# Experts' second product by Strassen's scheme in two of three super chunks

## The chip, the cores and the metric

The kernel runs on one core of one Trainium2 chip. The metric is the device time of one execution in microseconds (us); the median of three runs of the kernel before is 2102.27 us (2100.63 to 2102.86).

## The reference, cut to what matters

Feature attention (4 batches, 8 heads, 576 positions) gives x, a chain of matrix products turns x into a new x of 2304 tokens by 512, and a mixture of eight experts makes the output. The change touches the experts alone:

```python
P = np.exp(logits)                       # gate, then 8 rounds of row and column scaling
out = np.zeros((N, D), dtype=np.float32)  # N 2304 tokens, D 512, 8 experts of width F 1024
for e in range(E):
    h = np.maximum(x @ w1[e], 0.0)       # first product
    ye = h @ w2[e]                       # second product
    out += P[:, e:e + 1] * ye
```

## The kernel before, in words

Every float32 operand is kept as a high and a low part in the fast float32 format of TensorE, and each product of two tiles is three matmuls (high with high, high with low, low with high), written by `mm3` (L86). The attention, the product chain and the gate's logits fill the first 564 us; the experts fill the rest.

The 2304 tokens are cut into three super chunks (s) of 768 tokens, in two column halves of 384. Inside a super chunk the eight experts (e) follow each other, and in an expert four units (p). A unit makes two row blocks of 128 hidden values, p and p + 4, for 768 tokens.

The first product of a unit already uses Strassen's scheme (Winograd's form): seven products of 384 columns in place of eight, each of six matmuls (`product` in `unit`, L732). A product lands in a PSUM bank (pool `ph`, five banks); VectorE adds it into one of four 128 x 384 tiles of a buffer `c` (L749; two such buffers, pool `ut`); ScalarE copies the first one. `h_split` (L728) then takes relu and splits it into `hH` (ScalarE) and `hL` (VectorE).

The second product of an expert runs when its four units are done: for each of six tiles of 128 tokens, eight row blocks by three matmuls of 512 columns into a bank of pool `py`, 144 matmuls in all. VectorE multiplies the result by the gate and adds it to the output tile `oacc` (L857).

Weights: in the first super chunk `load_w1` and `prep_w1` (L482, L491) fetch the seven combinations of w1 for each unit, split them, and store the split form in a DRAM scratch (`W1S`, 1.79 MB a unit, counted in 1024s). In the two later super chunks that scratch is loaded again, into one of three buffers. w2 is loaded and split anew for every expert of every super chunk (`load_w2` L710, `split_w2` L719): ScalarE makes the high part, VectorE or GpSimd the low part. The x operands of the first product are made once per super chunk (`load_x`, `prep_x`, L450 and L454).

The order of instructions on each engine is planned when the program is built. The planner takes, of what it holds to be ready, the instruction that stands first in the program text; the adds of a product are moved 60 places forward. Engines run their lists in order, so an instruction that waits holds up all behind it. All large DMAs are issued by SP, in its own list.

Of the kernel before, what the change touches and what calls it, by code (L numbers as in the profile page):

```python
# [15 lines left out]
    Xl="v", Xs="g", Wt="v", Wh="a", Wl="gv", W2h="a", W2l="vg",  # L16
# [11 lines left out]
def kernel(  # L28
# [80 lines left out]
    W1S = [scr.tile([P, 2, 7, 2 * P], F32, name=f"w1s{i}") for i in range(NE * FT2 // 2)]  # L109
# [340 lines left out]
    def load_x(s):  # L450
        rawX[s] = rx.tile([P, KT, 2 * N1], F32, name=f"rx{s}", tag="rx")
        nc.sync.dma_start(rawX[s], XS[s])

    def prep_x(s):  # L454
        r = rawX.pop(s)
        a, b = slice(0, N1), slice(N1, 2 * N1)
        a11, a12, a21, a22 = r[:, 0:2, a], r[:, 2:4, a], r[:, 0:2, b], r[:, 2:4, b]
# [24 lines left out]
    def load_w1(u):  # L482
        if u < len(units):
# [4 lines left out]
            nc.sync.dma_start(rawW1[u][:, 0:3], moe2_w1[e, p][:, 1:4])  # L488
            nc.sync.dma_start(rawW1[u][:, 3:7], W1T[u])

    def prep_w1(u):  # L491
        if u >= len(units):
            return
        n = u % len(W1S)
        if u >= len(W1S):
            pool = wc1c[0] if u % 3 == 2 else wc1
            hl = pool.tile([P, 2, 7, 2 * P], F32R, name=f"w1_{u}", tag="hl")
            nc.sync.dma_start(f32(hl), W1S[n])
            WC[u] = hl[:, 0], hl[:, 1]
            return  # L500
        r = rawW1.pop(u)
        hl = wc1.tile([P, 2, 7, 2 * P], F32R, name=f"w1_{u}", tag="hl")
        hi, lo = hl[:, 0], hl[:, 1]
        for i, c in enumerate((slice(0, 3), slice(3, 7))):
            copy("Wh", hi[:, c], r[:, c], 2 * u + i)
            subtract("Wl", lo[:, c], r[:, c], f32(hi[:, c]), 2 * u + i)
        nc.sync.dma_start(W1S[n], f32(hl))
        WC[u] = hi, lo
# [188 lines left out]
    with c4:  # L697
        hp = sbuf(c4, "hp")
        ut = sbuf(c4, "ut", 2)
        op = sbuf(c4, "op")  # L700
        sk = sbuf(c4, "sk", 2)
        st = sbuf(c4, "st", 2)
        wp = sbuf(c4, "wp")
        ph_p = c4.enter_context(tc.tile_pool(name="ph", reuse_waits="tile", bufs=5, space=PSUM))
        py_p = c4.enter_context(tc.tile_pool(name="py", reuse_waits="tile", bufs=2, space=PSUM))
# [4 lines left out]
        def load_w2(u):  # L710
            if u < len(units):
# [3 lines left out]
                    t, moe2_w2[e, 2 * p * P : 2 * (p + 1) * P, :].rearrange("(j p) d -> p j d", p=P)  # L715
                )
                rawW2[u] = t

        def split_w2(u):  # L719
            s, e, p = units[u]  # L720
            t = rawW2.pop(u)
            hi = wp.tile([P, 2, DM], F32R, name=f"w2h{u}", tag=f"h{p}")
            lo = wp.tile([P, 2, DM], F32R, name=f"w2l{u}", tag=f"l{p}")
            copy("W2h", hi, t, u)
            subtract("W2l", lo, t, f32(hi), u)
            W2[p] = hi, lo

# [4 lines left out]
        def unit(u, between):  # L732
# [3 lines left out]
            B11, B21, B22, T1, T2, T3, T4 = range(7)  # L736

            def product(x, i, *adds):
                ps = ph_p.tile([P, N1], F32, name=f"p{x}{u}", tag="ph")
                (wh, wl), (xh, xl) = WC[u], XC[x]  # L740
                for kt in range(2):
                    k = slice(kt * P, (kt + 1) * P)
                    mm3(ps, wh[:, i, k], wl[:, i, k], xh[:, kt], xl[:, kt], kt == 0, kt == 1)
# [11 lines left out]
            product("s1", T1, (c22, c21), (c12, c12))  # L755
            product("a12", B21, (c11, c11))
            product("a22", T4, (c21, c21))
# [56 lines left out]
        for u, (s, e, p) in enumerate(units):  # L814

            if u + 1 < len(W1S):
                prep_w1(u + 1)
                load_w1(u + 2)
            if u + 2 == len(W1S):
                c6.close()  # L820
                wc1c.append(sbuf(c6, "wc1c", 1, "left"))
            if u + 2 >= len(W1S):
                prep_w1(u + 2)
# [5 lines left out]
            if e == 0 and s + 1 < NSC:  # L829
                load_x(s + 1)  # L830
            if e == NE - 1 and s + 1 < NSC:
                prep_x(s + 1)
            for tt in range(2 * N1 // P):
# [7 lines left out]
                for n, ft in enumerate(fts):  # L841
                    hi, lo = W2[ft // 2]
                    mm3(ps, hH[ft][:, tcs], hL[ft][:, tcs], hi[:, ft % 2], lo[:, ft % 2], n == 0, n == FT2 - 1)
# [14 lines left out]
                if e == NE - 1:  # L858
                    nc.sync.dma_start(out[t * P : (t + 1) * P, :], o)

# [75 lines left out]
```

## Time and profile before

| | |
|---|---|
| median of three runs | 2102.27 us |
| profiled execution, whole | 2102.98 us |
| its span, first to last instruction | 2101.2 us |
| TensorE busy | 2051.8 us (98%), 11877 matmuls |
| VectorE busy | 1131.7 us (54%) |
| ScalarE busy | 597.6 us (28%) |
| GpSimd busy | 361.4 us (17%) |
| granted TensorE clock, mean | 0.994 |
| DMA | 345 MB, 164 GB/s over the span |

Busy time of an engine is the time in which at least one of its instructions was in flight. Matmuls overlap, so the time from one start to the next tells what a matmul costs, and not its own duration. A row of a timeline names the engine, the line, the tile written and the tiles read; "x2" means two such instructions merged. A DMA share of 1.00 means that all 16 engines were at work.

### The profile page before, as it was taken

What the parts mean: (1) busy time and instruction counts of PE and PEld (TensorE: products, weight loads), DVE (VectorE), ACT (ScalarE), POOL (GpSimd) and SP (SyncE); (2) the same over time, 40 slices, a digit from 0 to 9 for tenths busy, and PEclk for the clock granted to TensorE, in tenths of its full rate; (3) what the DMA queues carried; (4) which work ended last, traced back from release to release, by engine and by line L of the source; (5) the groups of instructions that cost most, each with busy time, mean ns of one, the idle gap of its engine ahead of it and who ended that gap; (6) DMA issues with size and microseconds to landing.
All of it is one profiled execution on the core that took longest, in us unless ns stands there. A gap on an engine that the chain in (4) does not pass through costs nothing.

```text
span 2101.2 us, 28910 instructions
## 1 busy us (share of the span) xinstructions
PE 2051.8 (98%) x11877; PEld 1819.2 (87%) x11877; DVE 1131.7 (54%) x1718; ACT 597.6 (28%) x979; POOL 361.4 (17%) x268
## 2 busy tenths in 40 slices
PE   7999889999989999999999999999999999999999
PEld 6667689999978888889888999888999888999887
DVE  7765853343586554666554555444565443555443
ACT  6765532222333322233221122111132211122211
POOL 3433331221422211122120000000010000000000
PEclk9999999999999999999999999999999999999999
DMA  6432345554574545665464444333455333444330
GB/s 214 146 119 84 131 141 156 183 158 156 215 270 170 204 167 221 240 226 191 168 228 154 171 180 166 129 110 147 170 190 192 124 114 142 170 180 179 120 117 31
DMA packets 78531, 345.44 MB, mean 164 GB/s; under 512 B 7488, under 2 KB 11456, under 8 KB 65728
## 3 DMA queue, kind: packets, MB, share of 16 engines
q1 hardware_dynamic: 77808, 342.95, 45.7%
q8 instruction: 93, 1.52, 0.3%
q10 hardware_dynamic: 592, 0.66, 0.1%
q14 instruction: 38, 0.31, 0.0%
HBM read 256.54 MB, written 87.03 MB: 164 GB/s over the span
## 4 chain that ended last, share of the span: by engine, by line
PE 83%; DVE 6%; ACT 3%; issue 3%; POOL 3%; DMA 2%; ACTq 0%; SPq 0%; DVEq 0%; POOLq 0%
PE py L89 13%; PE py L87 13%; PE py L88 13%; PE ps L87 6%; PE ps L88 5%; PE ps L89 5%; PE pa L89 4%; PE pa L88 4%; PE pa L87 4%; PE ab L89 3%; PE ab L87 3%; PE ab L88 3%; DMA r<-in_moe_w_dram 1%; PE px L89 1%; PE px L88 1%
## 5 line engine op out<-in xcount | busy, mean ns | idle before, releaser
L89 PE MATMUL py<-w2h,hL 128*128 128x512 f32 x1152 | 457.5, 397 | 0.6 <-DVE hL L730 0.4
L87 PE MATMUL py<-w2h,hH 128*128 128x512 f32 x1152 | 456.7, 396 | 0.6 <-DVE o L855 0.6
L88 PE MATMUL py<-w2l,hH 128*128 128x512 f32 x1152 | 456.8, 397 | 0.0
L857 DVE SCALAR_TENSOR_TENSOR o<-py,Pw,o 128x512 f32<-128x512 f32 x126 | 94.6, 751 | 451.9 <-PE py L89 451.9
L99 POOL TENSOR_TENSOR w2l<-r,w2h 128x1024 fp32r<-128x1024 f32 x48 | 116.2, 2421 | 1106.3 <-ACT w2h L96 1093.0
L749 DVE TENSOR_TENSOR c<-c,ps 128x384 f32<-128x384 f32 x480 | 256.0, 549 | 88.1 <-PE ps L89 81.3
L96 ACT CAST w2h<-r 128x1024 fp32r<-128x1024 f32 x96 | 101.0, 1052 | 701.1 <-PE py L89 613.1
L89 PEld LDWEIGHTS py<-w2h,hL 128*128 128x128 f32 x1152 | 216.8, 188 | 56.5 <-DVE hL L730 4.3
L87 PEld LDWEIGHTS py<-w2h,hH 128*128 128x128 f32 x1152 | 217.0, 188 | 52.8 <-DVE o L855 1.0
L88 PEld LDWEIGHTS py<-w2l,hH 128*128 128x128 f32 x1152 | 217.0, 188 | 51.5
L730 DVE SCALAR_TENSOR_TENSOR hL<-c,hH 128x768 fp32r<-128x768 f32 x192 | 234.4, 1237 | 27.7 <-ACT hH L729 25.9
L729 ACT ACTIVATE hH<-c 128x768 fp32r<-128x768 f32 x192 | 158.0, 843 | 294.9 <-DVE c L749 273.1
L87 PE MATMUL ab<-XH,wH 128*128 128x384 f32 x384 | 131.2, 342 | 8.6 <-DVE wH L96 8.6
L89 PE MATMUL ab<-XH,wL 128*128 128x384 f32 x384 | 131.3, 342 | 1.1 <-DVE wL L99 1.1
L88 PE MATMUL ab<-XL,wH 128*128 128x384 f32 x384 | 130.7, 340 | 0.0
L749 DVE TENSOR_TENSOR c<-c,pa 128x384 f32<-128x384 f32 x192 | 102.2, 549 | 17.4 <-PE pa L89 16.0
L647 POOL TENSOR_TENSOR cL<-a,cH 128x384 fp32r<-128x384 f32 x48 | 58.3, 1215 | 232.2 <-ACT cH L646 232.1
L99 DVE TENSOR_TENSOR w2l<-r,w2h 128x1024 fp32r<-128x1024 f32 x48 | 60.3, 1257 | 58.7 <-ACT w2h L96 58.6
L99 POOL TENSOR_TENSOR w<-r,w 128x768 fp32r<-128x768 f32 x32 | 65.8, 2058 | 130.1 <-ACT w L96 114.0
L96 ACT CAST w<-r 128x768 fp32r<-128x768 f32 x64 | 59.8, 938 | 95.4 <-DMA r<-in_moe_w_dram 30.4
L645 DVE TENSOR_TENSOR a<-ab,a 128x384 f32<-128x384 f32 x48 | 26.7, 557 | 104.9 <-PE ab L89 104.9
L87 PEld LDWEIGHTS ab<-XH,wH 128*128 128x128 f32 x384 | 72.9, 190 | 10.2 <-DVE wH L96 8.3
(174 smaller groups left out, 3842.8 us busy)
## 6 DMA issues: line engine op xcount, KB each, us to landing
w<-w1s SPq DMA_DIRECT2D x64, 1792.0 KB, 7.5
w1s<-w SPq DMA_DIRECT2D x32, 1792.0 KB, 6.6
r<-in_moe_w_dram SPq DMA_DIRECT2D x96, 512.0 KB, 3.5
rw<-in_w_dram SPq DMA_DIRECT2D x32, 512.0 KB, 3.8
tr<-in_moe_w_dram SPq DMA_DIRECT2D x32, 512.0 KB, 4.4
w1t<-tt SPq DMA_DIRECT2D x32, 512.0 KB, 5.1
r<-w1t SPq DMA_DIRECT2D x32, 512.0 KB, 8.2
r<-in_moe_w_dram SPq DMA_DIRECT2D x32, 384.0 KB, 7.7
```

What stands on the lines that cost most here:

```text
L87: nc.tensor.matmul(ps, aH, bH, start=start, stop=False)
L88: nc.tensor.matmul(ps, aH, bL, start=False, stop=False)
L89: nc.tensor.matmul(ps, aL, bH, start=False, stop=stop)
L96: (e.copy if e is nc.scalar else e.tensor_copy)(out, src)
L99: engine(key, i).tensor_tensor(out, a, b, ALU.subtract)
L645: behind = nc.vector.tensor_tensor(cc, ab[1], a_sb, ALU.mult).ins
L647: nc.gpsimd.tensor_tensor(l, cc, f32(h), ALU.subtract)
L729: nc.scalar.activation(hH[ft], src, AF.Relu)
L730: nc.vector.scalar_tensor_tensor(hL[ft], src, 0.0, f32(hH[ft]), ALU.max, ALU.subtract)
L749: nc.vector.tensor_tensor(o, t, ps, ALU.add)
L857: nc.vector.scalar_tensor_tensor(o, ps, Pw[:, t, e : e + 1], o, ALU.mult, ALU.add)
```

## The change

In the second and third super chunks the second product is computed by Strassen's scheme as well: h is the left factor, cut in four blocks (two halves of the tokens, two halves of the hidden rows), w2 is the right factor. Seven groups of products on half-size blocks replace eight. A group is four units by three token tiles by three matmuls of 256 columns. VectorE and ScalarE form the combinations of h after each unit (`operands`); the combinations of w2 are formed and split once, in the first super chunk (`split_w2`), stored in a DRAM scratch `W2S`, and loaded group by group in the later ones (`load_t`, three buffers). Partial results are copied out by ScalarE (`keep`) and added to the output by VectorE (`gated`). The first super chunk itself computes as before, with w2's row blocks paired p and p + 4. The split w1 is kept in two tiles (five and two combinations) with two buffers of each in place of three whole ones; `back_w1` reloads each part as soon as the unit two earlier has finished reading it. The x of the third super chunk is loaded into the two `c` buffers.

The core of the diff:

```diff
-    Xl="v", Xs="g", Wt="v", Wh="a", Wl="gv", W2h="a", W2l="vg",
+    Xl="v", Xs="g", Wt="v", Wh="a", Wl="vgg", W2h="a", W2l="vg", Tw="v", Th="a", Tl="v",
...
+    W2S = [scr.tile([P, 7, FT2 // 2, 2, DH], F32, name=f"w2s{i}") for i in range(NE)]
...
+    def back_w1(u, i):
+        if len(W1S) <= u < len(units):
+            if i == 1:
+                w1_tiles(u)
+            nc.sync.dma_start(f32(WC[u][1 - i]), W1S[u % len(W1S)][i])
...
         def split_w2(u):
...
             copy("W2h", hi, t, u)
             subtract("W2l", lo, t, f32(hi), u)
             W2[p] = hi, lo
+            for k, j, d in ((K11, 0, d0), (K21, 1, d0), (K22, 1, d1)):
+                nc.sync.dma_start(W2S[e][:, k, p], f32(w[:, j, :, d]))
+            add("Tw", b11, b12, b11, ALU.subtract)
+            add("Tw", b12, b22, b12, ALU.subtract)
+            add("Tw", b22, b11, b22, ALU.subtract)
+            add("Tw", b21, b21, b22, ALU.add)
+            x = tp.tile([P, 4, 2, DH], F32R, name=f"t2_{u}", tag="t")
+            copy("Th", x[:, :, 0], t, u)
+            subtract("Tl", x[:, :, 1], t, f32(x[:, :, 0]), u)
+            for i, k in enumerate((KT1, KT3, KT4, KN2)):
+                nc.sync.dma_start(W2S[e][:, k, p], f32(x[:, i]))
...
-            product("a12", B21, (c11, c11))
             product("a22", T4, (c21, c21))
-            h_split(p, c[:, 0:2].rearrange("p a n -> p (a n)"))
+            back_w1(u + 2, 1)
+            product("a12", B21, (c11, c11))
+            yield c
             product("s4", B22, (c12, c12))
-            h_split(p + NP, c[:, 2:4].rearrange("p a n -> p (a n)"))
+            back_w1(u + 2, 0)
+            yield c
...
+        def split(u, key, n, src, relu):
...
+            if relu:
+                nc.scalar.activation(hi, src, AF.Relu)
+                nc.vector.scalar_tensor_tensor(lo, src, 0.0, f32(hi), ALU.max, ALU.subtract)
+            else:
+                nc.scalar.copy(hi, src)
+                nc.vector.tensor_tensor(lo, src, f32(hi), ALU.subtract)
+        def operands(u):
+            for i, c in enumerate(products(u, lambda n: bank(n)[:, 0:N1], lambda: None)):
+                if i == 0:
+                    nc.scalar.activation(c22, c22, AF.Relu)
+                    nc.scalar.activation(c21, c21, AF.Relu)
+                    HS[p, K11], = split(u, "a", 1, c[:, 0:1], True)
+            HS[p, K21], HS[p, KT4] = split(u, "b", 2, c[:, 2:4], True)
+            nc.vector.tensor_tensor(c22, c21, c22, ALU.add)
+            stt(c21, c11, 0.0, c21, ALU.max, ALU.subtract)
+            stt(c11, c11, 0.0, c22, ALU.max, ALU.subtract)
+            stt(c12, c12, 0.0, c11, ALU.max, ALU.add)
+            HS[p, K22], HS[p, KT1] = split(u, "d", 2, c[:, 2:4], False)
+            HS[p, KN2], HS[p, KT3] = split(u, "e", 2, c[:, 0:2], False)
...
+            operands(u)
+            if p < NP - 1:
+                load_t(u, p)
+                continue
...
+            def group(k, dst, fresh=()):
+                for q in range(NP):
+                    H, L = HS[q, k]
+                    T = TK[k][:, q]
+                    for i in range(NI):
+                        nc.tensor.matmul(dst[i], H[:, c], T[:, 0], start=f, stop=False, skip_group_check=True)
+                        nc.tensor.matmul(dst[i], H[:, c], T[:, 1], start=False, stop=False, skip_group_check=True)
+                        nc.tensor.matmul(dst[i], L[:, c], T[:, 0], start=False, stop=l, skip_group_check=True)
+                if k + 3 < 7:
+                    load_t(u, k + 3)
...
+            group(K11, a, (0, 2))
+            keep(0, a)
+            group(K21, b0, range(NI))
+            group(KT4, d, (0,))
+            keep(2, d)
+            group(KT1, b1)
+            keep(3, b1)
+            group(KN2, a)
+            keep(1, a)
+            gated(1, [mt[:, i, 2:4] for i in range(NI)], True)
+            gated(0, [mt[:, i, 0:2] for i in range(NI)], True)
+            group(K22, b1)
+            gated(0, [x.rearrange("p (q d) -> p q d", q=2) for x in b])
+            store(0)
+            group(KT3, a)
+            gated(1, [x.unsqueeze(1).to_broadcast([P, 2, DH]) for x in a])
+            store(1)
```

`keep` is three ScalarE copies of 128 x 256, `gated` three VectorE operations on 128 x 512. The accumulators of an expert take six banks of a pool of seven (`bk`) that the first product's banks come from too. `split(u, key, n, ...)` splits n tiles of 384 columns in one instruction on each engine.

## Rows read from the trace of the kernel before

**Rows 1.** The page's first part: busy us (share of the span), instructions.
```profile
PE 2051.8 (98%) x11877; PEld 1819.2 (87%) x11877; DVE 1131.7 (54%) x1718; ACT 597.6 (28%) x979; POOL 361.4 (17%) x268
```
**Rows 2.** The page's chain that ended last, shares by engine.
```profile
PE 83%; DVE 6%; ACT 3%; issue 3%; POOL 3%; DMA 2%; ACTq 0%; SPq 0%; DVEq 0%; POOLq 0%
```
**Rows 3.** Busy by stretch: super chunk 1 from its third expert; chunks 2 and 3.
```profile
core 0: us, PE busy (x) PEld busy (x) DVE busy (x) ACT busy (x) POOL busy (x), PEclk, DMA share, GB/s
708.40:1090.92 382.52, 380.62 (x1873) 336.56 (x1872) 223.30 (x293) 116.36 (x148) 81.56 (x38) 1.00 0.57 209
1090.92:2097.20 1006.28, 1006.28 (x4993) 900.04 (x4991) 488.37 (x710) 199.85 (x262) 81.17 (x34) 1.00 0.40 147
```
**Rows 4.** The same of one later expert: its first product, its second.
```profile
1216.67:1245.82 29.15, 29.15 (x169) 29.15 (x168) 22.86 (x35) 9.27 (x14) 4.81 (x2) 1.00 0.72 261
1245.82:1279.56 33.74, 33.74 (x146) 27.13 (x146) 7.36 (x9) 2.96 (x4) 0.00 (x0) 1.00 0.16 55
```
**Rows 5.** Timeline (start us, us): a matmul, the next weight load, the next matmul.
```profile
2094.93 0.39 PE L87 MATMUL py<-w2h,hH 128*128 128x512 f32 x1
2094.94 0.19 PEld L88 LDWEIGHTS py<-w2l,hH 128*128 128x128 f32 x1
2095.16 0.40 PE L88 MATMUL py<-w2l,hH 128*128 128x512 f32 x1
```
**Rows 6.** Timelines of PEld and PE: six weight loads and 128-column matmuls.
```profile
87.42 0.81 PEld L203 LDWEIGHTS dt<-ident,d 128*128 128x128 f32 x6
87.65 0.82 PE L203 MATMUL dt<-ident,d 128*128 128x128 f32 x6
```
**Rows 7.** Timeline of VectorE in one expert's first product.
```profile
904.12 1.22 DVE L99 TENSOR_TENSOR w2l<-r,w2h 128x1024 fp32r<-128x1024 f32 x1
905.26 1.01 DVE L749 TENSOR_TENSOR c<-c,ps 128x384 f32<-128x384 f32 x2
...
917.96 0.96 DVE L730 SCALAR_TENSOR_TENSOR hL<-c,hH 128x768 fp32r<-128x768 f32 x1 [0.45 <-ACT hH L729]
918.84 0.55 DVE L749 TENSOR_TENSOR c<-c,ps 128x384 f32<-128x384 f32 x1
```
**Rows 8.** Groups by line: busy us, mean ns, idle before.
```profile
L857 DVE SCALAR_TENSOR_TENSOR o<-py,Pw,o 128x512 f32<-128x512 f32 x126 | 94.6, 751 | 451.9 <-PE py L89 451.9
L96 ACT CAST w2h<-r 128x1024 fp32r<-128x1024 f32 x96 | 101.0, 1052 | 701.1 <-PE py L89 613.1
```
**Rows 9.** Who waited for whom: us in total, times, longest.
```profile
DVE hL L730 <- ACT hH L729: 25.9, 55, 2.1
```
**Rows 10.** Busy by stretch, tile py, then tile ps (first product).
```profile
607.00:619.60 12.60, 11.85 (x48) 8.89 (x48) 0.00 (x0) 1.00 0.97 364
...
619.60:635.00 15.40, 8.16 (x42) 7.29 (x42) 3.78 (x7) 1.00 0.51 185
```
**Rows 11.** DMA of 900 to 964: packets, MB, share; then two loaded stretches.
```profile
q1 hardware_dynamic: 2816, 13.11, 56.2%
...
920.00:924.00 4.00, 4.00 (x25) 4.00 (x24) 4.00 (x8) 0.00 (x0) 0.00 (x0) 1.00 1.01 331
1232.00:1238.00 6.00, 6.00 (x36) 6.00 (x35) 4.73 (x9) 1.50 (x3) 0.00 (x0) 1.00 1.00 413
```
**Rows 12.** DMA issues: count, KB each, median us to landing.
```profile
w1s<-w SPq DMA_DIRECT2D x32, 1792.0 KB, 6.6
...
rx<-xs SPq DMA_DIRECT2D x3, 1536.0 KB, 7.7
```
**Rows 13.** Tiles of x's preparation, 1500 to 1610: ns min/median/max, start us.
```profile
L96 ACT CAST a11h<-rx x1: 840/840/840, 1554.9 to 1554.9; 128x768 fp32r<-128x768 f32 x1
...
L99 DVE TENSOR_TENSOR s4l<-xs,s4h x1: 957/957/957, 1569.8 to 1569.8; 128x768 fp32r<-128x768 f32 x1
```
**Rows 14.** Timeline of the end.
```profile
2097.24 0.75 DVE L857 SCALAR_TENSOR_TENSOR o<-py,Pw,o 128x512 f32<-128x512 f32 x1 [4.87 <-PE py L89]
2098.02 0.33 SPq L859 DMA_DIRECT2D out_dram<-o  x1
```

More of the change, by code (lines that the diff above doesn't have):

```diff
@@ L107 @@
     XS = [scr.tile([P, KT, 2 * N1], F32, name=f"xs{i}") for i in range(NSC)]
-    W1S = [scr.tile([P, 2, 7, 2 * P], F32, name=f"w1s{i}") for i in range(NE * FT2 // 2)]
+    W1S = [
+        [scr.tile([P, 2, n, 2 * P], F32, name=f"w1s{i}_{n}") for n in (2, 5)]
+        for i in range(NE * FT2 // 2)
+    ]
+    DH = DM // 2
+    W2S = [scr.tile([P, 7, FT2 // 2, 2, DH], F32, name=f"w2s{i}") for i in range(NE)]
     W1T = [scr.tile([P, 4, 2 * P], F32, name=f"w1t{i}") for i in range(NE * FT2 // 2)]
@@ L448, in add, with load_x @@
         engine(key, i).tensor_tensor(out, a, b, op)
-    def load_x(s):
-        rawX[s] = rx.tile([P, KT, 2 * N1], F32, name=f"rx{s}", tag="rx")
-        nc.sync.dma_start(rawX[s], XS[s])
+    def load_x(s, tiles=None):
+        if tiles is None:
+            r = rx.tile([P, KT, 2 * N1], F32, name=f"rx{s}", tag="rx")
+            nc.sync.dma_start(r, XS[s])
+            tiles = r[:, 0:2], r[:, 2:4]
+        else:
+            for i, r in enumerate(tiles):
+                nc.sync.dma_start(r, XS[s][:, 2 * i : 2 * i + 2])
+        rawX[s] = tiles
     def prep_x(s):
@@ L710, in load_w2 @@
         def load_w2(u):
-            if u < len(units):
+            if u < len(W1S):
                 s, e, p = units[u]
@@ L730, in h_split, with products @@
             nc.vector.scalar_tensor_tensor(hL[ft], src, 0.0, f32(hH[ft]), ALU.max, ALU.subtract)
-        def unit(u, between):
+        def products(u, bank, between):
             s, e, p = units[u]
@@ L755, in unit, with bank @@
             product("s1", T1, (c22, c21), (c12, c12))
+            product("a22", T4, (c21, c21))
+            back_w1(u + 2, 1)
             product("a12", B21, (c11, c11))
-            product("a22", T4, (c21, c21))
-            h_split(p, c[:, 0:2].rearrange("p a n -> p (a n)"))
+            yield c
             product("s4", B22, (c12, c12))
-            h_split(p + NP, c[:, 2:4].rearrange("p a n -> p (a n)"))
+            back_w1(u + 2, 0)
+            yield c
+        def unit(u, between):
+            s, e, p = units[u]
+            def bank(name):
+                return ph_p.tile([P, N1], F32, name=name, tag="ph")
+            for i, c in enumerate(products(u, bank, between)):
+                h_split(p + i * NP, c[:, 2 * i : 2 * i + 2].rearrange("p a n -> p (a n)"))
         m1 = sk.tile([P, 1], F32, name="m1", tag="m1", bufs=1)
@@ L859, with bank, load_t @@
                     nc.sync.dma_start(out[t * P : (t + 1) * P, :], o)
+        c8.close()
+        hs = sbuf(c4, "hs")
+        tk = sbuf(c4, "tk", 3)
+        bk_p = c4.enter_context(tc.tile_pool(name="bk", reuse_waits="tile", bufs=7, space=PSUM))
+        HS, TK = {}, {}
+        def bank(name):
+            return bk_p.tile([P, DM], F32, name=name, tag="b")
+        def load_t(u, k):
+            s, e, p = units[u]
+            TK[k] = tk.tile([P, NP, 2, DH], F32R, name=f"t{s}_{e}_{k}", tag="t")
+            nc.sync.dma_start(f32(TK[k]), W2S[e][:, k])
@@ new lines, in split @@
+        def split(u, key, n, src, relu):
+            hi, lo = (
+                hs.tile([P, n, N1], F32R, name=f"{key}{x}{u}", tag=f"{key}{x}{units[u][2]}") for x in "hl"
+            )
+            if relu:
+                nc.scalar.activation(hi, src, AF.Relu)
+                nc.vector.scalar_tensor_tensor(lo, src, 0.0, f32(hi), ALU.max, ALU.subtract)
+            else:
+                nc.scalar.copy(hi, src)
+                nc.vector.tensor_tensor(lo, src, f32(hi), ALU.subtract)
+            return [(hi[:, i], lo[:, i]) for i in range(n)]
```

135 lines of the change are left out of this document (93 added, 42 removed).

## The prediction

> **What bounds the kernel now.** I read the page's engine shares first: TensorE is busy 98% of the span, VectorE 54%, ScalarE 28%, GpSimd 17% [rows 1]. The chain of waits says the same: 83% of it lies on PE [rows 2]. The busy times by stretch show where this holds. From 1090.92 on, the second and third super chunks, PE is busy in every one of 1006.28 us at full clock, while VectorE has 488 and DMA a share of 0.40; from 708.40 to 1090.92, the last six experts of the first super chunk, PE lacks 1.9 us of 382.5 [rows 3]. So the sixteen experts of the two later super chunks take 62.89 us each, and only matmul time counts there: 29.15 us of first product (168 matmuls) and 33.74 us of second product (144 matmuls), the latter with VectorE busy 7.4 us alone [rows 4]. A matmul of 384 columns costs 29.15 / 168 = 173.5 ns, one of 512 columns 33.74 / 144 = 234.3 ns.
>
> **The new second product.** An expert has 7 groups x 4 units x 3 token tiles x 3 = 252 matmuls of 256 columns in place of 144 of 512. No long run of that shape stands in the trace, so I bound it. Below: weight loads of 128 columns with matmuls of 128 columns; six take 0.82 us, five starts and a last one of 0.27, thus 0.11 us each [rows 6]. A load overlaps the matmul before it: it starts 0.01 us after that one and its own matmul follows 0.22 us later [rows 5]; 110 ns is the least that a pair has shown. Above: what 384 columns cost beyond the 160 ns of their columns at 2.4 GHz, 13.5 ns, added to 106.7 ns: 120 ns. Between lie the straight line through 173.5 and 234.3, which gives 112.7, and 173.5 x 256 / 384 = 115.7. I take 114.5, near the middle of these two, as 384 is the nearest row. 252 x 114.5 = 28.85 us, 4.89 less than 33.74; times 16 it is **-78.2 us** (-96 at 110 ns, -56 at 120).
> The Trainium skill ("TensorE: Matmul & The Clock Gate", Back-to-back issue gap) has N / 2.4 + 2.5 ns, thus 109 ns and about -100 us. By that rule 384 and 512 columns would cost 162.5 and 215.8 ns; the trace has 173.5 and 234.3 [rows 4], so the measurement decides and I stay above it.
>
> **VectorE and ScalarE in the later super chunks.** Successive starts give VectorE 0.46 us for 384 elements (two take 1.01, one 0.55), 0.88 for 768 and 1.14 for 1024 [rows 7]; the line through the first two gives 0.32 for 256 and 0.60 for 512, where the gate's operation is listed at 0.75 alone [rows 8]. A unit keeps its seven adds (3.22 us). In place of two splits of 768 it has one split of 384, three of 768 and four combinations of 384: 0.46 + 2.64 + 1.84 = 4.94 us. Gating doubles to twelve operations, 7.2 us. An expert needs 4 x 8.16 + 7.2 = 39.8 us of VectorE in 58.0 us: hidden on the average, but not in its place. When PE ends unit 3 at 29.15 us it goes on with the first group and needs unit 3's first operand 27 matmuls later, at 32.2. By then VectorE must have done 28 adds, the operands of three units and one split, 12.9 + 14.8 + 0.46 = 28.2 us, and it cannot begin before the second product lands at 2.3 us (the earlier expert's last three gates, 1.8 us, fit in front): 30.5 us, a margin of 1.7. Every one of the sixteen splits waits for a ScalarE instruction first; where such waits show now they are 25.9 us in 55, 0.47 each [rows 9]. If half of them show, 3.8 us, PE waits 3.8 - 1.7 = 2.1 us at each expert: **+33.6 us**. Bounds: 0, where other adds fill these waits or the planner moves the next expert's products ahead of the group that isn't ready, as it did at 607 to 635 (48 matmuls of a second product, then 42 first-product matmuls of tile ps) [rows 10]; and 16 x 0.47 - 1.7 = 5.8 us, +93. Queued behind a late split on VectorE are the next adds, and seven PSUM banks take seven products until PE waits for those.
> Taken away there are four ScalarE casts of w2 (1.05 us each [rows 8]), two VectorE and two GpSimd splits and 2.1 MB of loads per expert; PE hid all of it, so it earns nothing but room. ScalarE's new work (about 4 us of splits, relus and copies a unit and twelve short copies an expert) stays under half of the time.
> DMA there: four units of 1.835 MB and seven combinations of 1.05 MB, 14.7 MB in 60 us, 245 GB/s, where a loaded stretch moved 413 [rows 11]. I cost it at nothing: a reload of w1 is issued 9.4 us before its unit starts, and three buffers hold the combinations. On SP a combination's load waits for the end of a group; behind it stand only loads that are due later. If the rate fell to 245 it would show at once.
>
> **The first super chunk.** Per unit there are four sums of 256 and a split of 1024 on VectorE (4 x 0.32 + 1.14 = 2.4 us), one cast of 1.05 us on ScalarE, and seven stores of 0.262 MB. VectorE has 223 us in 382 now [rows 3]; the added 9.7 us per expert fit into the second product. DMA is the tighter resource: one expert moves 13.11 MB and takes 56.2% of 64 us [rows 11], 36.0 us. The stores add 28 x 0.262 = 7.34 MB, at the same rate 20.1 us: 56 of 63.75 us, 88%. What is issued in 29.6 us of first product then takes well over 40, and the rest drains in the second product. All of it goes through SP in one order: raw weights for later units stand behind stores. The tile of combinations has one buffer, so the cast of the next unit waits on ScalarE for four stores to land (a w1 store takes 6.6 us to land now [rows 12]); queued behind it are the copy of the next product and the relus, and five PSUM banks cover 5 x 1.04 us. A store that finds 5 us of others before it lands after about 11.6, 4.3 us more than the 7.3 us of a unit; I take that this shows at every second expert: 2.2, with 0.1 for VectorE 2.3 us per expert, x 8 = **+18.4 us** (0 to 45; 0 if the planner put these casts in the second product).
>
> **Ends.** The third super chunk's x needs both `c` buffers, free some 7 us into the last second product; it lands 7.7 us later [rows 12], and the preparation lasts 16 us (1554.9 to 1570.7) [rows 13]: 31 against 28.85, +2. At the end three gates stand in place of one, +1.2 us after 2097.24, and three output stores of one [rows 14]: +2. The change of pools after the first super chunk waits for its last readers: 1 to 5, I take 2. Together **+6 us** (2 to 15).
>
> **Sum**: profiled execution 2102.98 (span 2101.2 and 1.8 around it) - 78.2 + 33.6 + 18.4 + 6 = 2082.8. That execution is 0.7 above the median of 2102.27, so 2082 us.
>
> **Rivals.**
> A, all is hidden: no wait for VectorE and none for DMA, -78.2 + 6: 2030 us. For it: the averages (VectorE 69%, DMA 88%) and the interleaving of rows 10. Against it: both peaks fall in the first product, where VectorE has 22.9 of 29.15 us already [rows 4].
> B, VectorE sets each expert's end: all sixteen splits wait and nothing is moved ahead, 5.8 us x 16 = 93 in place of 33.6: 2142 us. It decides from 3.4 us per expert on, eleven of sixteen waits. For it: instructions run in a fixed order, so each wait is paid by all behind it. Against it: adds of the next unit lie between the splits.
> C, slower by the first super chunk's DMA: an expert there needs 20.45 MB, with stores in pieces of 1 and 2 KB. A loaded stretch moved 331 GB/s, another 413 [rows 11]; at 331 it takes 61.8 of 63.75 us. At 290 it is 70.5 us, +6.8 x 8 = 54 in place of 18.4: 2118 us. It decides below 298 GB/s, 4.8 us an expert. Against it: 34 us of second product for the backlog.
> D, the weight load sets the pace: one load before the next, 188 ns as listed for a load of 0.19 us [rows 5], 252 x 0.188 = 47.4 us per expert, +218 us, VectorE hidden: 2345 us. Rows 4 speak against it: 173.5 ns is already less.
> The Trainium skill (same page, Measured speedup vs the span model) says that a load overlaps a running matmul only if the row groups differ, which would bring D or worse; in rows 5 it overlaps with all 128 rows in both, so by the trace that rule doesn't hold here.
>
> **Chances.** Forecast 46% (its own range 2058 to 2101), A 15%, B 14%, C 18%, D 2%, mixtures between them 5%. The range of 8 in 10 runs from 2030, A, to 2130, past C and to B's lower half. About 0.2%, 4.2 us, is what a measurement of this kernel can tell from no change. Faster: 0.44 of the forecast, 0.15 of A, 0.07 of lighter cases of B, C and the mixtures, 0.66; same 0.08; slower 0.26.
>
> **What would show it.** Right: matmuls of 256 columns every 113 to 116 ns in the later super chunks; experts of 59 to 62 us there; PE waits of 1 to 3 us an expert for splits on VectorE; experts of the first super chunk 65 to 67 us, DMA share near 0.9. Wrong: a pace over 120 ns, waits over 3.4 us an expert, or a first super chunk more than 39 us longer.

## The result and the profile after

The changed kernel takes 2074.46 us (median of four runs, 2073.11 to 2076.48) beside 2102.57 for the kernel before on the same chip: a ratio of 0.9868 (95% interval 0.9851 to 0.9886), 28.1 us less. The forecast was 2082, 20 less. The nearness hides two wrong terms of opposite sign, as the rows show.

The page's first part and its chain after the change, to hold against [rows 1, 2]:

```profile
PE 2005.9 (97%) x13605; PEld 1874.4 (90%) x13605; DVE 1421.1 (68%) x2326; ACT 776.0 (37%) x1427; POOL 294.8 (14%) x268
...
PE 56%; DVE 9%; issue 3%; DMA 2%; ACT 1%; POOL 0%; SPq 0%; POOLq 0%; DVEq 0%; ACTq 0%
```

TensorE's busy time fell by 46 us only, though it has 1728 more matmuls of half the columns in place of the long ones. Busy times by stretch, after: four experts of the first super chunk (the fourth to the seventh), its last one, most of the second super chunk, most of the third, and one expert.

```profile
core 0: us, PE busy (x) PEld busy (x) DVE busy (x) ACT busy (x) POOL busy (x), PEclk, DMA share, GB/s
779.74:1042.97 263.23, 256.53 (x1249) 223.72 (x1248) 196.21 (x273) 94.80 (x128) 56.37 (x41) 1.00 0.87 312
1042.97:1113.87 70.90, 65.74 (x313) 57.09 (x312) 50.19 (x71) 22.59 (x31) 13.11 (x8) 0.98 0.73 265
1113.87:1575.81 461.94, 461.94 (x3253) 461.76 (x3252) 331.46 (x566) 168.61 (x317) 0.64 (x1) 1.00 0.71 253
1594.26:2068.90 474.64, 474.64 (x3364) 474.64 (x3363) 338.10 (x577) 168.62 (x319) 0.00 (x0) 1.00 0.68 240
...
1173.35:1232.69 59.34, 59.34 (x422) 59.34 (x421) 42.47 (x73) 21.14 (x40) 0.00 (x0) 1.00 0.70 248
```

The reader is to see two kernels in one. From 1113.87 on TensorE is busy in all of the time (but for the change of super chunk between the third and fourth row) although VectorE's share there rose from 0.49 [rows 3] to 0.72: no wait for VectorE shows. In the first super chunk TensorE lacks 6.7 of 263.2 us, 65.8 us an expert beside 63.75 before [rows 3].

An expert of the later super chunks takes 59.35 us (before 62.89), from the start of one to that of the next. The timeline of PE (start us, us) in one second product gives the pace:

```profile
1274.76 0.28 PE L987 MATMUL b<-t,dh 128*128 128x256 f32 x1
1274.88 0.28 PE L988 MATMUL b<-t,dh 128*128 128x256 f32 x1
1275.00 0.28 PE L989 MATMUL b<-t,dl 128*128 128x256 f32 x1
```

They start every 120.0 ns. With 168 matmuls at 173.3 and 252 at 120.0 an expert is 29.11 + 30.24 = 59.35 us, all of it.

Where the 28 us come from, by the starts of the stages in both traces: sixteen experts 3.54 us shorter, -56.6; the first super chunk 547.15 us (566.72 to 1113.87) in place of 526.47 (564.45 to 1090.92), +20.7; the change to the third super chunk +5.5; from the start of the last matmul to the end 5.78 in place of 4.36 us, +1.4; the stage ahead, whose code is unchanged, +2.3 (it ended between 562.4 and 566.7 us in the runs below). Sum -26.7; the two profiled executions differ by 26.5.

### The profile page after: what moved, and what is told of

Same layout as the page of the kernel before. It is cut to its first block, busy times and chain, and to the rows that moved or that the text cites. A ratio compares the mean times of both kernels' runs of the same rounds, so it can differ in the third digit from the quotient of the medians.

```text
span 2074.7 us, 34057 instructions
## 1 busy us (share of the span) xinstructions
PE 2005.9 (97%) x13605; PEld 1874.4 (90%) x13605; DVE 1421.1 (68%) x2326; ACT 776.0 (37%) x1427; POOL 294.8 (14%) x268
## 4 chain that ended last, share of the span: by engine, by line
PE 56%; DVE 9%; issue 3%; DMA 2%; ACT 1%; POOL 0%; SPq 0%; POOLq 0%; DVEq 0%; ACTq 0%
PE ps L89 5%; PE ps L87 5%; PE ps L88 5%; PE pa L89 4%; PE pa L88 3%; PE pa L87 3%; PE py L89 3%; PE py L88 3%; PE py L87 3%; PE b L989 3%; PE b L988 3%; PE b L987 3%; DVE c L789 3%; PE a L987 2%; PE a L989 2%
## 5 line engine op out<-in xcount | busy, mean ns | idle before, releaser
L99 POOL TENSOR_TENSOR w<-r,w 128x256 fp32r<-128x256 f32 (+2 forms) x80 | 115.0, 1449 | 389.1 <-ACT w L96 310.6
L87 PE MATMUL py<-w,hH 128*128 128x512 f32 x384 | 154.3, 403 | 5.8 <-DVE o L904 2.2
L96 ACT CAST w<-r 128x1024 fp32r<-128x1024 f32 (+2 forms) x128 | 96.5, 778 | 164.2 <-DMA r<-in_moe_w_dram 79.9
L89 PE MATMUL py<-w,hL 128*128 128x512 f32 x384 | 154.8, 404 | 2.9 <-DVE hL L770 2.7
L88 PE MATMUL py<-w,hH 128*128 128x512 f32 x384 | 154.1, 402 | 3.0 <-POOL w L99 3.0
L1005 DVE SCALAR_TENSOR_TENSOR o<-mt,Pw,o 128x512 f32<-128x512 f32 x84 | 61.4, 786 | 122.4 <-ACT mt L995 122.4
L987 PE MATMUL b<-t,dh 128*128 128x256 f32 x384 | 108.7, 283 | 0.0
L988 PE MATMUL b<-t,dh 128*128 128x256 f32 x384 | 108.7, 283 | 0.0
L989 PE MATMUL b<-t,dl 128*128 128x256 f32 x384 | 108.7, 283 | 0.0
L906 DVE SCALAR_TENSOR_TENSOR o<-py,Pw,o 128x512 f32<-128x512 f32 x42 | 31.4, 749 | 102.6 <-PE py L89 102.6
L667 DVE TENSOR_TENSOR a<-ab,a 128x384 f32<-128x384 f32 x48 | 26.7, 557 | 104.0 <-PE ab L89 104.0
L87 PEld LDWEIGHTS py<-w,hH 128*128 128x128 f32 x384 | 73.4, 191 | 24.0 <-DVE o L904 2.5
L89 PEld LDWEIGHTS py<-w,hL 128*128 128x128 f32 x384 | 73.4, 191 | 24.0 <-DVE hL L770 6.7
L88 PEld LDWEIGHTS py<-w,hH 128*128 128x128 f32 x384 | 73.8, 192 | 20.8 <-POOL w L99 3.7
```

The costliest lines, as they stand in the source:

```text
L87: nc.tensor.matmul(ps, aH, bH, start=start, stop=False)
L88: nc.tensor.matmul(ps, aH, bL, start=False, stop=False)
L89: nc.tensor.matmul(ps, aL, bH, start=False, stop=stop)
L96: (e.copy if e is nc.scalar else e.tensor_copy)(out, src)
L99: engine(key, i).tensor_tensor(out, a, b, ALU.subtract)
L987: nc.tensor.matmul(dst[i], H[:, c], T[:, 0], start=f, stop=False, skip_group_check=True)
```

## The experiments

### How long a matmul of 256 columns must take

Run alone behind the last group, 48 matmuls of each of eleven shapes, some 74 us more in all.

```diff
+        with tc.issue_after(behind):
+            for n, m in ((512, 128), (448, 128), (384, 128), (320, 128), (256, 128), (192, 128), ...
+                for j in range(48):
+                    w = (h0, h1, h2)[j % 3][0][:, 0:m]
+                    nc.tensor.matmul(ps[0:m, 0:n], w, mov[:, 0:n], start=True, stop=True)
```

> The changed kernel with streams of matmuls appended at the end, behind the last matmul of the second product: 48 each of 512, 448, 384, 320, 256, 192 and 128 columns with weights of 128 columns, then 512, 384, 256 and 128 columns with weights of 32 columns. It tells what makes a 256-column matmul 120 ns in the changed kernel, where I had taken 114.5. Theory: a cost of about 13.3 ns per matmul beside its columns, whatever the weights: 234, 200, 173.3, 146.7 and 120 ns down to 256 columns, the same with weights of 32 columns at 512, 384 and 256; at 192 and 128 columns the weight load sets the pace, near the 110 ns of rows 6, and only there do narrow weights help. Rival: the load of 128 weight columns itself takes 120 ns: then 192 and 128 columns stay at 120, and 256 columns with weights of 32 fall to 107 to 110 ns. The time itself grows by about 85 us of appended matmuls.

2148.7 us. PE's busy time, one stretch for each shape in the order of the loop: 512, 448, 384, 320, 256, 192, 128 columns with 128 columns of weights, then 512, 384, 256 and 128 with 32.

```profile
core 0: us, PE busy (x), PEclk, DMA share, GB/s
2065.48:2076.39 10.91, 10.91 (x48) 1.00 0.21 74
2076.39:2086.12 9.73, 9.73 (x50) 1.00 0.00 0
2086.12:2094.44 8.32, 8.32 (x49) 1.00 0.00 0
2094.44:2101.47 7.03, 7.03 (x49) 1.00 0.01 2
2101.47:2107.23 5.76, 5.76 (x50) 1.00 0.00 0
2107.23:2112.57 5.34, 5.34 (x50) 1.00 0.02 3
2112.57:2117.90 5.33, 5.33 (x50) 1.00 0.00 0
2117.90:2129.01 11.11, 11.11 (x50) 1.00 0.00 0
2129.01:2137.33 8.32, 8.32 (x49) 1.00 0.01 2
2137.33:2142.99 5.66, 5.66 (x50) 1.00 0.00 0
2142.99:2145.81 2.82, 2.82 (x50) 1.00 0.00 0
```

Divided by 48: 227, 202.7, 173.3, 146.5, 120.0, 111.3 and 111.0 ns; with 32 columns of weights 231, 173.3, 118 and 60 ns (the last stretch ends where its last matmul starts, so it is divided by 47). At 2.4 GHz (the granted clock is 1.00 in every row) the columns alone are 213.3, 186.7, 160.0, 133.3 and 106.7 ns of the first five: 13.1 to 13.3 ns stay on top of them at 256, 320 and 384 columns, but 16.0 at 448 and 14.0 at 512, so one constant fits only the narrower three. With a quarter of the weights 384 columns cost the same 173.3, 256 cost 2 ns less and 512 cost 4 more, so at most a small part of the 13.3 ns is the load's. At 192 and 128 columns the load of 128 columns sets a floor of 111 ns, which at 128 columns falls to 60 with the small load. So 120.0 is the shape's own cost, not something around it.

### Is VectorE's wait hidden by the order on TensorE?

After the change the planner puts 11 matmuls of the second group ahead of the last five of the first one, those that need the operand split last. Here the second group may not begin before the first one's end.

```diff
-            group(K11, a, (0, 2))
+            behind = group(K11, a, (0, 2))
             keep(0, a)
-            group(K21, b0, range(NI))
+            with tc.issue_after(behind):
+                group(K21, b0, range(NI))
```

> The changed kernel, but no matmul of the second group may stand ahead of the last matmul of the first group in TensorE's order. In the changed kernel 11 of them do, in every later expert, while unit 3's first low part is made, and TensorE never waits. Theory: these 11 x 120 ns cover the wait that my VectorE account foresaw; without them TensorE waits about 1.3 us (1.0 to 2.1) in each of 16 experts: +21 us (16 to 34), 2095 us. Rival: VectorE is in time anyway (the margin of 1.7 us was too small): no change, 2074 within 4 us.

2081.18 us (ratio to before 0.9905, 0.9891 to 0.992): 6.7 us over the changed kernel; the experts take 59.87, 0.52 more each. PE's waits from 1140 to 1560 (us in total, times, longest):

```profile
PE a L989 <- DVE al L930: 2.0, 7, 0.3
```

The wait is there, at the operand that the prediction named, but it costs 0.5 us an expert (0.3 of it idle in this view) and not 2.1; and the order that the planner chose covers all of it. The sign of the expectation held, its size did not. What the prediction had too large are VectorE's own waits for ScalarE's half of a split. In the changed kernel, from 1180 to 1570, these are all that show:

```profile
DVE bl L930 <- ACT bh L929: 3.8, 7, 0.8
DVE el L933 <- ACT eh L932: 2.2, 7, 0.3
```

That is 0.9 us an expert, where the prediction counted 3.8.

### How much room VectorE has there

The low parts of two of the splits of 768 columns are written three times in each unit: 14.1 us more of VectorE in an expert.

```diff
-                nc.vector.tensor_tensor(lo, src, f32(hi), ALU.subtract)
+                for _ in range(1 + EXTRA):       # EXTRA = 2
+                    nc.vector.tensor_tensor(lo, src, f32(hi), ALU.subtract)
```

> The changed kernel with two splits of 768 elements of every unit in the later super chunks written three times by VectorE in place of once: 4 x 0.88 = 3.5 us more per unit, 14.1 per expert. VectorE is busy 42.6 of 59.35 us per expert now, so the sum would still fit. Theory (the place counts, as in my account): the extra work of units 0 to 2, 10.6 us, falls before the first operand of unit 3; TensorE waits 5 to 9 us at each expert, +80 to +145 us. Rival (the average counts, the planner finds other matmuls): at most 1 us per expert, under 2090 us.

2202.87 us (1.048, 1.0459 to 1.0501): 8.0 us for each of the sixteen experts, which now take 66.4 to 67.7 us. With 42.5 + 14.1 = 56.6 us of VectorE in 59.35 it would still fit on the average; it doesn't in its place. The busy times from 1163 to 1500, then the waits from 1140 to 1560, where PE had none before: PE for a bank that ScalarE's copy of a product frees, and that copy for the very splits that are written three times (`dl`).

```profile
1163.00:1500.00 337.00, 310.09 (x2106) 307.53 (x2106) 280.06 (x443) 106.97 (x202) 0.00 (x0) 0.95 0.60 219
...
ACT c L787 <- DVE dl L935: 59.5, 13, 4.9
...
PE a L989 <- ACT c L787: 37.6, 7, 5.4
```

Not all of the 8.0 us is waiting. PE is idle 26.9 of the 337 us, 5.4 us an expert; the other 2.6 go with the granted clock, which is 0.95 in this stretch and 1.00 in the changed kernel: it falls to the lower of its two levels (1.2 GHz) behind each of these waits.

So VectorE's place decides, not its average, as reckoned; but the margin was larger than the 1.7 us that I worked out: of the 10.6 us that the first three units add ahead of the group, 5.4 reach PE, which leaves some 5 us (an estimate from these two numbers).

### The first super chunk: stores or combinations?

One run leaves out 49 of the 56 MB of stores (counted in 1024s; the later super chunks read the first expert's combinations for all), another the sums, the cast and the split of the combinations, with all seven stores kept.

```diff
-                nc.sync.dma_start(W2S[e][:, k, p], f32(x[:, i]))
+                if e == 0:
+                    nc.sync.dma_start(W2S[0][:, k, p], f32(x[:, i]))
...
-            nc.sync.dma_start(f32(TK[k]), W2S[e][:, k])
+            nc.sync.dma_start(f32(TK[k]), W2S[0][:, k])
```

> The changed kernel, but only the first expert's combinations of w2 are stored, and every later load reads those: 49 of 56 MB of stores are left out of the first super chunk (the output is that of other weights). The first super chunk is 20.7 us longer than before. Theory: the queue of DMAs costs it (late raw weights, and casts that wait for stores): 12 to 20 us come back, 2055 to 2062 us, and the DMA share there falls from 0.85 to about 0.57. Rival: VectorE's extra work, slowed beside GpSimd's splits, costs it: no more than 5 us come back, 2070 to 2075.

```diff
-            add("Tw", b11, b12, b11, ALU.subtract)
...
-            subtract("Tl", x[:, :, 1], t, f32(x[:, :, 0]), u)
-            for i, k in enumerate((KT1, KT3, KT4, KN2)):
-                nc.sync.dma_start(W2S[e][:, k, p], f32(x[:, i]))
+            for k, j, d in ((KT1, 0, d1), (KT3, 1, d0), (KT4, 1, d1), (KN2, 0, d0)):
+                nc.sync.dma_start(W2S[e][:, k, p], f32(w[:, j, :, d]))
```

> The changed kernel with all seven stores per unit kept, but the four sums, the cast and the split of w2's combinations left out (the four stores take plain blocks of w2, so the output is not the reference's). It takes away 2.4 us of VectorE work per unit and 1 us of ScalarE, and the wait of the next cast for stores, and no DMA. Theory (the DMA queue costs the first super chunk its 20.7 us): at most 6 us come back, 2068 to 2075. Rival (VectorE and ScalarE): 12 to 20 us come back, 2055 to 2062.

Without the stores: 2086.08 us (0.9929, 0.9914 to 0.9943), 11.6 slower than with them; both expectations missed. The four experts of that stretch, with the DMA share down from 0.87:

```profile
776.63:1049.87 273.24, 262.12 (x1250) 229.69 (x1249) 194.46 (x273) 93.99 (x128) 70.36 (x41) 0.98 0.53 193
```

Without the combinations: 2055.7 us (0.9779, 0.9763 to 0.9795), 19 faster, at a DMA share of 0.91:

```profile
768.91:1026.56 257.65, 253.29 (x1249) 224.29 (x1248) 141.54 (x192) 78.52 (x112) 55.67 (x40) 1.00 0.91 318
```

So the time does not follow DMA: my theory of the first super chunk falls. What PE waited for most without the stores, 780 to 1114, and the timeline of one of the five (VectorE, GpSimd and PE, 857 to 864; the next two GpSimd splits left out):

```profile
PE ps L87 <- DVE c L791: 12.3, 5, 2.5
...
859.35 2.95 DVE L99 TENSOR_TENSOR w<-r,w 128x1024 fp32r<-128x1024 f32 x1
862.22 1.01 DVE L791 TENSOR_TENSOR c<-c,ps 128x384 f32<-128x384 f32 x2
...
858.24 2.97 POOL L99 TENSOR_TENSOR w<-r,w 128x1024 fp32r<-128x1024 f32 x1 [1.42 <-ACT w L96]
...
863.28 0.65 PE L87 MATMUL ps<-s2h,w 128*128 128x384 f32 x1 [2.48 <-DVE c L791]
```

A VectorE split of 1024 that takes 1.22 us elsewhere [rows 7] takes 2.95: it begins while a GpSimd split runs, and ends 1.09 us after that one has ended, at 861.21. The adds behind it free PE's banks, and PE stands 2.48 us for them. That made a new theory, and the changed kernel's own trace has the same thing at the combinations (two sums on VectorE that follow each other, and GpSimd's split):

```profile
909.20 2.50 DVE L453 TENSOR_TENSOR r<-r 128x256 f32<-128x256 f32 x1
911.73 0.42 DVE L453 TENSOR_TENSOR r<-r 128x256 f32<-128x256 f32 x1
...
908.93 2.48 POOL L99 TENSOR_TENSOR w<-r,w 128x1024 fp32r<-128x1024 f32 x1 [10.79 <-ACT w L96]
```

The sum that begins 0.27 us after GpSimd's split takes 2.50 us and ends 0.29 us after that split; the next one takes 0.42. So VectorE waits here for GpSimd to end, and is not slowed to another pace: the 0.97 us a sum in the expectations below is the mean of four sums, of which one waited. Over the first super chunk 32 of the 128 sums began while a GpSimd instruction ran; each of them ended 0.28 to 0.29 us after it and took 0.43 to 2.51 us. The other 96 took 0.36 to 0.43.

### Take GpSimd's splits away

First w2's low parts on VectorE alone, then w1's too. VectorE gets more work, not less.

```diff
-    ... Wl="vgg", W2h="a", W2l="vg", ...
+    ... Wl="vgg", W2h="a", W2l="v", ...      # first run
+    ... Wl="v", W2h="a", W2l="v", ...        # second run
```

> The changed kernel with w2's low parts in the first super chunk made by VectorE for every unit, in place of VectorE and GpSimd in turn. VectorE gets 2 x 1.14 us more per expert there, GpSimd loses 2 x 2.4 us. In the changed kernel a 256-element sum takes 0.97 us of VectorE beside such a GpSimd split and 0.41 alone, and one 1024-element split took 3.38 us in place of 1.22. Theory: the first super chunk pays for VectorE time stretched beside GpSimd: 4 to 12 us come back, 2062 to 2070. Rival: it pays for the amount of VectorE work: slower by 2 to 10 us, 2076 to 2084.

> As the kernel before it, and w1's low parts all on VectorE too (0.33 + 0.60 us more per unit), so that GpSimd has no split left in the first super chunk. Theory (stretched VectorE time): 6 to 16 us come back against the changed kernel, 2058 to 2068. Rival (amount of VectorE work, 6 us more per expert): 2080 to 2095.

2063.59 us (0.9816, 0.9802 to 0.9831) and 2056.23 (0.9783, 0.9768 to 0.9798): 11 and 18 us faster than the change. VectorE's groups of 780 to 1094 or 1114 (busy us, mean ns), first of the changed kernel, then of the second run:

```profile
L789 DVE TENSOR_TENSOR c<-c,ps 128x384 f32<-128x384 f32 x100 | 53.0, 547 | 1.4 <-PE pa L89 0.5
L453 DVE TENSOR_TENSOR r<-r 128x256 f32<-128x256 f32 x79 | 52.2, 662 | 1.0
L770 DVE SCALAR_TENSOR_TENSOR hL<-c,hH 128x768 fp32r<-128x768 f32 x40 | 44.2, 1111 | 1.4 <-ACT hH L769 1.3
...
L99 DVE TENSOR_TENSOR t<-r,t 128x1024 fp32r<-128x1024 f32 x20 | 32.1, 1605 | 1.0 <-ACT t L96 1.0
```

```profile
L789 DVE TENSOR_TENSOR c<-c,ps 128x384 f32<-128x384 f32 x94 | 50.0, 549 | 3.6 <-PE ps L89 2.6
...
L770 DVE SCALAR_TENSOR_TENSOR hL<-c,hH 128x768 fp32r<-128x768 f32 x39 | 36.8, 952 | 0.3 <-ACT hH L769 0.2
L453 DVE TENSOR_TENSOR r<-r 128x256 f32<-128x256 f32 x75 | 31.6, 421 | 0.8
L99 DVE TENSOR_TENSOR t<-r,t 128x1024 fp32r<-128x1024 f32 x19 | 23.2, 1221 | 3.1 <-ACT t L96 2.7 <-DMA w2s<-w 0.3
```

The sums fell from 662 to 421 ns, the splits from 1605 to 1221 and 1111 to 952. The adds from a bank, with one input in PSUM, stayed at 547 and 549: only operations that read two tiles of SBUF are held up.
The Trainium skill ("SBUF — State Buffer", Who interferes with whom) says just this: a VectorE instruction with two SBUF inputs contends with a GpSimd instruction that reads SBUF, one with at most one, outside the 2-port modes, does not. The trace agrees, with these numbers.

### Did this cost anything before, and what is left?

The same edit in the kernel before; and the changed kernel without the combinations and without GpSimd's splits; and without the stores and without GpSimd's splits.

```diff
-    ... Wl="gv", W2h="a", W2l="vg",
+    ... Wl="v", W2h="a", W2l="v",
```

> The kernel before the change with its GpSimd splits (half of W's and half of W2's low parts) on VectorE, nothing else. Theory: VectorE operations stretched beside GpSimd (0.97 against 0.41 us for 128x256 sums) hurt only where VectorE has little room; the kernel before waits about 1 us an expert in its first super chunk (periods 63.2 to 64.1 against 62.9 later), so it gains at most 1 us an expert there and a few us in the stage ahead: 2090 to 2100 us. Then some 10 of the 18 us that this edit gives after the change belong to the combinations. Rival: the gain has nothing to do with the combinations and comes in full here too: 2102 minus 18 = 2084. Other rival: the edit only helps with the combinations: 2100 to 2103.

> The four sums, the cast and the split of the combinations in the first super chunk are left out (all seven stores stay, of uncombined weights), and no split runs on GpSimd. It tells whether the combinations' own VectorE and ScalarE work costs anything once nothing stretches it. Theory: no, it then fits beside the matmuls: the same as with the combinations and no GpSimd, 2052 to 2058 us (2056.2 there). Rival: the work itself delays TensorE by over 1 us an expert even alone: 2040 to 2048.

> The run without 49 of the 56 MB of stores (the second and third super chunk read the first expert's combinations for all) came out 11.6 us slower than the changed kernel; here the same, with all splits of low parts on VectorE. Theory: the loss there was one VectorE split in each expert that ran beside GpSimd's and took 2.95 us instead of 1.22 ahead of the sum that TensorE's next bank waits for (2.5 us waited, five times); without GpSimd the experts of the first super chunk go at 62.9 to 63.2 us, and the time is within 4 us of the 2056 us that the kernel with stores and without GpSimd splits took. Rival: the earlier casts and sums, let go by the missing stores, are in the wrong place in VectorE's order whatever GpSimd does: the experts stay at 65 us or more and the time is 2068 us or more.

The kernel before gains too: 2087.92 us (0.9941, 0.9924 to 0.9957), 12.7 less, between my theory and its rival. Its own VectorE rows show where; the split of h, 777 to 1094, in the kernel before and with the edit:

```profile
L730 DVE SCALAR_TENSOR_TENSOR hL<-c,hH 128x768 fp32r<-128x768 f32 x40 | 58.0, 1458 | 10.9 <-ACT hH L729 10.6
```

```profile
L730 DVE SCALAR_TENSOR_TENSOR hL<-c,hH 128x768 fp32r<-128x768 f32 x40 | 39.3, 994 | 0.4 <-ACT hH L729 0.4
```

So of the 18.2 us that the edit gives after the change, 12.7 were there before it, and 5.5 came with the change.
Without combinations and GpSimd's splits: 2047.11 us (0.9744, 0.973 to 0.9759), 9.1 below the same with combinations, so my theory that they then cost nothing fell, and its rival gave the right size at the wrong place: four experts take 251.83 us here, 62.96 each, full pace with them or without, and the difference lies in the first and the last expert (PE idle there: 2.5 and 6.0 us with them, 1.4 and 1.4 without; the granted clock of the last expert is 0.95 with them, 1.00 without).

```profile
769.06:1020.89 251.83, 251.83 (x1249) 224.94 (x1248) 155.07 (x232) 80.43 (x112) 0.00 (x0) 1.00 0.93 326
```

The four runs of the changed kernel also tell what the combinations have to do with GpSimd: its splits cost 8.6 us without them (2055.7 against 2047.11) and 18.2 with them.
Without stores and GpSimd's splits: 2056.24 us (0.9787, 0.977 to 0.9803), the same as with the stores, 2056.23. The stores cost nothing, and the loss of the run without them was GpSimd's.

### The change of super chunk, and both edits together

By the starts of the experts the change from the second to the third super chunk costs 5.5 us over the pace; it lies between 1575.81 and 1594.26. PE is idle 3.5 us of that stretch, and the granted clock over it is 0.91. ScalarE's timeline there, of the changed kernel (idle before it, and what ended it, in brackets):

```profile
1588.25 0.83 ACT L96 CAST s4h<-xs 128x768 fp32r<-128x768 f32 x1 [2.92 <-POOL xs L453]
1588.99 0.36 ACT L995 COPY mt<-a 128x256 f32<-128x256 f32 x1
```

The copies that free a bank stood behind a cast that waited for GpSimd's sum of the next x; PE waited 3.0 us for them. One run moves these copies forward in the planner's eyes; another does that and takes GpSimd's splits away.

```diff
-                for i in range(NI):
-                    nc.scalar.copy(mt[:, i, j], src[i])
+                with tc.high_priority(500):
+                    for i in range(NI):
+                        nc.scalar.copy(mt[:, i, j], src[i])
```

> The changed kernel, with ScalarE's copies of the partial sums moved 500 places forward in the planner's order. At the end of the second super chunk TensorE waited 3.0 us for such a copy, which stood behind a cast of the next x that itself waited 2.9 us for GpSimd. Theory: that wait goes, 2 to 3 us come back (2071 to 2073), the rest of the 5.5 us there stays, as it hangs on loads. Rival: the casts of x then come later and the next products wait for them instead: no change, 2074 to 2076.

> Both mended places together: the splits of the weights' low parts on VectorE alone (no GpSimd split, as in the run that measured 2056.2 us), and the copies that keep a block issued ahead of other ScalarE work (as in the run that measured 2071.6, where the gap at the boundary of the second and third super chunk fell from 5.5 to 1.4 us). Theory: the two are at different places, the stretched VectorE beside GpSimd in the first super chunk and one copy behind a cast at the boundary, so they add: 2056.2 minus 3 to 4 gives 2052 to 2053 us. Rival: the kept copies issued early delay casts that the weights wait for, and part of one gain is lost: 2055 to 2060.

Alone 2071.6 us (0.9851, 0.9835 to 0.9868): by its times not apart from the change, but the change of super chunk costs 1.3 us in place of 5.5 in the trace, and the wait for `mt` is gone. Together 2051.74 us (0.9767, 0.9753 to 0.9782), the best version run that computes all, some 23 us below the changed kernel. Its four experts of the first super chunk:

```profile
680.89:932.38 251.49, 251.49 (x1250) 224.93 (x1249) 194.04 (x314) 94.94 (x128) 0.00 (x0) 1.00 0.90 325
```

PE is busy in all of it beside a DMA share of 0.90 and VectorE at 0.77, 62.87 us an expert. What is left of the loss lies at the ends of the super chunk. In its last expert a gate that frees a bank stands on VectorE behind the split of the next x, which waits for ScalarE, and that for GpSimd's sum (VectorE, ScalarE, PE, 1061 to 1068):

```profile
1065.00 0.96 DVE L99 TENSOR_TENSOR s2l<-xs,s2h 128x768 fp32r<-128x768 f32 x1 [2.56 <-ACT s2h L96]
...
1066.74 1.40 DVE L906 SCALAR_TENSOR_TENSOR o<-py,Pw,o 128x512 f32<-128x512 f32 x2
...
1064.13 0.83 ACT L96 CAST s2h<-xs 128x768 fp32r<-128x768 f32 x1 [7.34 <-POOL xs L453]
...
1067.54 0.80 PE L87 MATMUL py<-w,hH 128*128 128x512 f32 x1 [5.98 <-DVE o L906]
```

An own buffer for the next x, and a second one for the combinations' tile, are left untried.

## Why the prediction came out near, step by step

**The sum: luck.** The gain of the matmuls was put 21.6 us too high and the wait for VectorE 33.6 too high, and the two nearly cancel. With either one put right alone the forecast would have been 2104 or 2048.

**The pace of 256 columns: mis-sized.** The step "173.5 x 256 / 384 = 115.7 ... I take 114.5, near the middle of these two" failed. The measure is 120.0, the upper bound of the same paragraph: columns at 2.4 GHz plus 13.3 ns a matmul. The term is -56.6 us and not -78.2. I had the sentence that gives 120 and passed it over, because the straight line through 173.5 and 234.3 gave less. Alone, 512 columns cost 227 ns, 14 over their columns; in this kernel's second product they cost 7 ns more, for a reason that no run here shows, and that made the line too steep.

**VectorE in the later super chunks: wrong by the whole term.** "PE waits 3.8 - 1.7 = 2.1 us at each expert" gave +33.6; the trace has 0. Forced into the written order it is 0.5 us an expert, so three quarters of the error are in the account of the waits (half of sixteen at 0.47, 3.8 us, where 0.9 show) and one quarter in the order, which the prediction had named as the reason for its lower bound. With 14.1 us more of VectorE work a wait comes ahead of the same group, 5.4 us an expert: the place was right.

**The first super chunk: the size right, the cause wrong.** 2.3 us an expert were said, 18.4 in all; 2.1 are measured in the experts of its middle, 20.7 in all. Forecast rows came true as well (experts of 65 to 67 us, DMA share 0.87), which shows how little a confirmed symptom proves: with 49 MB of the stores left out the time rose, and with all of them and no GpSimd split it fell by 18. The step "the cast of the next unit waits on ScalarE for four stores to land" describes a wait that is there but costs nothing; what costs in the middle experts is VectorE held up by GpSimd's splits, up to 2.5 us for a sum that takes 0.42 alone. The prediction took the combinations' work as hidden, with durations from rows without GpSimd beside them (and a sum takes 0.46 us from start to start even so, not the 0.32 of its line). The sign of it was in the trace of before: the split that takes 0.96 us in [rows 7] took 1458 ns on the average. The four middle experts lose 8.2 us, and without GpSimd's splits nothing is left of that. The rest of the 20.7, 12.5 us, lies at both ends of the super chunk, and GpSimd does not explain that. The whole super chunk without its splits on either side (the run with both edits, then the kernel before with the edit):

```profile
564.53:1092.60 528.07, 512.87 (x2518) 454.81 (x2517) 399.45 (x702) 192.16 (x258) 8.64 (x4) 0.99 0.87 317
564.70:1075.98 511.28, 507.67 (x2518) 452.26 (x2516) 321.50 (x513) 158.30 (x198) 10.50 (x5) 1.00 0.59 219
```

The change still costs 16.8 us there, though four experts in a row take 251.5 and 253.5. PE is idle 15.2 and 3.6 us, nearly all in the first two experts and the last, and the granted clock is 0.99 and 1.00. With the combinations' work left out too the super chunk takes 519.9 us, so some 8 of the 16.8 go with that work. The last expert's wait is shown above; the first two experts I haven't taken apart, and what makes the other 8 to 9 us stays open.

**Ends.** +6 was said, 5.5 + 1.4 = 6.9 measured, and the stage ahead moved by 2.3 in the run that was profiled. The third super chunk's x is late, as said, but not by its landing: a cast in front of a copy on ScalarE makes 3.0 of the 5.5.

**Rivals.** A (2030, all hidden) was nearest in mechanism for the later super chunks: with the true pace its sum is 2103 - 56.6 + 6 = 2052. The combined version comes out there, though by another sum: it also gets back what GpSimd cost the kernel before, and still loses at the ends of the first super chunk. B decides only with 14 us more work. C falls: the stores cost nothing. D falls: the loads overlap, 120.0 ns a pair. (The rule that the prediction names beside D stands in the Trainium skill, "TensorE: Matmul & The Clock Gate", under The mechanism, which also lets a load into a background weight buffer go ahead of running matmuls.)

## What to carry to other kernels

Halving a matmul's columns doesn't halve its cost: add the fixed part of every matmul (13 ns here) before counting what a scheme with fewer flops but smaller tiles gives. An engine's durations from a trace hold for what ran beside it there; before work is added to VectorE, look for operations of the same form whose durations differ, and for what GpSimd did at the time. A helper engine that takes work off can cost more than it gives: here putting its splits back on the busier engine was worth 12.7 us before the change and 18.2 after it.

## What the hardware showed that was not expected

- A matmul in this format costs its columns at 2.4 GHz plus some 13.3 ns from 256 to 384 columns (120.0, 146.5, 173.3 ns), 16.0 at 448 and 14.0 at 512, and not less than 111 ns behind a load of 128 columns. With 32 columns of weights 384 columns cost the same. The Trainium skill ("TensorE: Matmul & The Clock Gate", Back-to-back issue gap) adds 2.5 ns in its formula for a matmul by itself, without its load; for this format the measurement decides.
- A VectorE operation on two SBUF tiles that begins while a GpSimd split runs doesn't end before it (2.50 us for a sum that takes 0.42, 2.95 for a split that takes 1.22); one with a PSUM input is not touched (547 and 549 ns).
- Behind PE's longer waits the granted clock falls to its lower level, 1.2 GHz, for a time: its mean is 0.95 from 1163 to 1500 where PE waits 5.4 us in each expert, 1.00 there without these waits.
- A DMA share of 0.90 for 250 us, 325 GB/s, went with TensorE at its full pace, 62.87 us an expert.
